# Gate weights by column halves, one visit for denominators and memory sums, and a new order of all work, in a mixed attention and feed-forward kernel

## The chip, the cores and the metric

The kernel runs on one core of one Trainium2 chip. TensorE (PE) multiplies, ScalarE (ACT) and VectorE (DVE) compute, GpSimd (POOL) and SyncE (SP) help, and DMA queues are fed by SP and ACT. The metric is the device time of one execution in microseconds, as the median of several runs. The inputs are bfloat16: a sequence of 2048 tokens with 512 features, four 512 by 512 attention weights, and the feed-forward weights of 512 by 1792, 512 by 1792 and 1792 by 512.

## The reference, cut to what matters

```python
q, k, v = ...                      # x @ wq, x @ wk, x @ wv, 32 heads of 16, 4 segments of 512 tokens
for s in range(4):
    p = softmax(q[s] @ k[s].T * 0.25 + causal_mask)
    a_dot = p @ v[s]
    pq = phi(q[s])                 # t + 1 where t > 0, else exp(t)
    a_mem = (pq @ M) / (pq @ z + 1e-6)
    o[s] = sigmoid(beta) * a_mem + (1 - sigmoid(beta)) * a_dot
    M = M + phi(k[s]).T @ v[s]
    z = z + phi(k[s]).sum(tokens)
a = o @ wo
b = (gelu(x @ w_gate) * (x @ w_up)) @ w_down
g = sigmoid((x * gate_w).sum(-1))
out = g * a + (1 - g) * b
```

In each segment of 512 tokens a causal softmax attention is mixed with a read of the memory M and its denominators z, which sum over earlier segments. A gated feed-forward runs on the same x, and a gate per token mixes the two results.

## The kernel before, in words

The work is cut into 1162 small tasks. Each names its engine, its instructions, and what it reads and writes. The string ORDER, written out at the end of the file, lists all tasks in one sequence. Every engine executes its own tasks in that sequence, and the emitter places a semaphore wait wherever a task reads what another engine wrote, or overwrites what another engine still reads. A digit behind a name says which of the four PSUM banks (or which turning buffer) the task takes, and `:a` or `:d` whether ACT or DVE copies a finished bank out. So the order decides where an engine has to wait.

For each segment s (0 to 3) these tasks matter here:

- `K`, `Q`, `V`, `G`, `U` with a segment and a tile number: dense products of x with the key, query, value, gate and up weights (line 483). A task is a pair of 512-column matmuls, `a` the first two input blocks and `b` the last two. Each product fills a bank that is then copied out by `Kev`, `Qev`, `Vev`, `Gev` (lines 475 and 476), by `gd` with the gelu in it (line 804), or multiplied on DVE by `h` (line 813). `gelu` (line 801) is the gelu of the first seven gate tiles in one instruction of 3584 columns.
- `st` with a segment, a quarter and a letter: a fill of the one score tile psX, which takes four of the eight banks, by four or eight small-tile matmuls side by side (line 634). `exp` (line 650, ACT) turns it into probabilities, `msk` (line 656, POOL) applies the causal triangle. The next fill may only start when that exponential has read psX.
- `pv` (line 687): 128 small-tile matmuls of probabilities and values into two banks, turned by DVE (`tp`, line 553), normalised (`pvp`), joined with the memory part and turned again (`ot`).
- `phq` and `phk`, each in three steps a, b, c (lines 493, 495, 496): the feature map phi of queries and keys on DVE, ACT and DVE. `ktr` (line 595) are four transposing DMAs, issued by SP, that bring the key features into token order.
- `mz` (line 602): 64 small-tile matmuls that form this segment's sums for M and z. `mzacc` (lines 608 and 609) adds them on DVE and scales M for the next read, `zq` (line 616) spreads z on POOL. `gate` (line 452) are 32 small matmuls for the token gates of two segments, in the same bank.
- `nz` (line 568): four small-tile matmuls for the denominators, in segments 1 to 3, turned by `tp_z` and inverted by `nzp`. `nd` (line 578) reads M into psX; four turns `tp_m` and four products `ndp` empty it, after which the next fill may start.
- `out`, `wev`, `wo`, `oev`, `dma` (lines 826 to 852): the down product, its scaling, the attention's output product, the sum, and the store. `chk` tests the softmax rows on DVE; `oksum` and `flag` join the tests, and every engine loads the flag at the end and branches on it.

The two kinds of visit of PE are of importance: dense products use the full array, while `st`, `pv`, `mz`, `nz`, `nd` and `gate` use tiles of 32 or 64 rows or columns.

Weights are loaded by SP in halves; each load names others that must have landed before it is issued. The gate weights `wg` come as `wg0` and `wg1`, each two of the four blocks of 128 input features with all 1792 columns, so a row of 3584 bytes each. The first two matmuls of a gate product read `wg0`, the last two `wg1`:

```python
ld_w("wg0", SP, wg[:, halves[0], :], wgr[:, halves[0], :], [("wg", 0)], 0.9, ["wq0"])
...
lambda i: [*x_of(s % R_XT, i), ("wg", i // 2)], 4)
```

At the start, PE runs `wake0` (five 512-column matmuls and three of 128 columns on constants) while the input lands, then turns x of the first segment (`xtr0_0` to `xtr0_3`, line 898), with one more filler, `wake1`, behind the second of these. `xev` copies the turned blocks out.

Of the kernel before, what the change touches and what calls it, by code (L numbers as in the profile page):

```python
# [12 lines left out]
ALU = mybir.AluOpType  # L13
# [239 lines left out]
def _build(es, nc, A_x, A_wq, A_wk, A_wv, A_wo, A_beta, B_w_gate, B_w_up, B_w_down, gate_w, out):  # L253
# [64 lines left out]
    def program(exact):  # L318
# [11 lines left out]
        def bk(s):  # L330
            return ("bank", s)
# [20 lines left out]
        def ld_w(name, eng, dst, src, writes, size, wait=()):  # L352
            load(name, eng, lambda e: e.dma_start(dst, src), writes, size=size, wait=[("ld", w) for w in wait])
# [20 lines left out]
        ld_w("wg0", SP, wg[:, halves[0], :], wgr[:, halves[0], :], [("wg", 0)], 0.9, ["wq0"])  # L374
        ld_w("wg1", SP, wg[:, halves[1], :], wgr[:, halves[1], :], [("wg", 1)], 0.9, ["wv"])
# [181 lines left out]
        def t_rows(ts, r):  # L557
            return tT[ts.i][:, :].rearrange("p (c r) -> p c r", r=32)[:, :, 0:r]
# [4 lines left out]
        def memory_read(s):  # L563
            b = s % 2
            for t0 in (0, 2):
                phi(s, "phq", qT[b], phq, t0, "qT")
            sl = Slot()
            one(f"nz{s}", PE, 0.24, [I(lambda e, c=c, sl=sl: e.matmul(  # L568
                BK[sl.i][32 * c:32 * c + 8, :], zq[:, c, :], phq[:, c, :], start=True, stop=True,
                tile_position=(0, 32 * c)), [("phq", c), ("zq",)], [bk(sl)]) for c in range(4)])  # L570
            ts = turn(f"{s}_z", lambda sl=sl: BK[sl.i][:, :], bk(sl))
            rv = rcm[:, :].rearrange("p (c r) -> p c r", r=8)
            one(f"nzp{s}", DVE, 1.15, [
                I(lambda e, rv=rv, ts=ts: e.tensor_scalar(rv, t_rows(ts, 8), EPS, None, ALU.add), [("tT", ts)], [("rcm",)]),
                I(lambda e: e.reciprocal(rcm[:, :], rcm[:, :]), [("rcm",)], [("rcm",)])])

            xs = Slot("X")
            one(f"nd{s}", PE, T_FILL, [I(lambda e, t=t, g=g, c=slot_of(t, g): e.matmul(  # L578
                XALL[quad(c), 512 * t:512 * t + 512], mzq[quad(g), c, :], phq[quad(g), c, :], start=True, stop=True,
                tile_position=(32 * g, 32 * c)), [("phq", slot_of(t, g)), ("mzq",)], [("X", xs)])  # L580
                for t in range(4) for g in range(4)], lat=0.27)
            for t in range(4):
                ts = turn(f"{s}_m{t}", lambda t=t: XALL[:, 512 * t:512 * t + 512], ("X", xs))
                f4 = lambda a: a.rearrange("p (c j e) -> p c j e", j=2, e=16)
                den = bass.AP(rcm, 2 * t, [[128, P], [8, 16], [1, 2], [0, 16]])
                one(f"ndp{s}_{t}", DVE, 0.61, [
                    I(lambda e, ts=ts, t=t, den=den: e.tensor_tensor(f4(omem[:, t, :]), f4(tT[ts.i][:, :]), den, ALU.mult),
                      [("tT", ts), ("rcm",)], [("omem", t)])])

        def memory_write(s):  # L590
            b = s % 2
            for t0 in (0, 2):
                phi(s, "phk", kT, phk, t0, "kT")
            for t in range(4):
                one(f"ktr{s}_{t}", SP, 1.3, [I(lambda e, t=t: e.dma_start_transpose(
                    phkt[:, :, t * 128:(t + 1) * 128], phk[:, t, :]), [("phk", t)], [("phkt", t)],
                    dma_sem=sem(f"s_k{s}_{t}"))]).size = 0.28

            sl = Slot()
            if s < 2:  # L600
                gate_products(s, sl)
            one(f"mz{s}", PE, 0.45, [I(lambda e, c=c, kt=kt, g=g, sl=sl: e.matmul(  # L602
                BK[sl.i][quad(g), 34 * c:34 * c + 34], phkt[:, kt, 128 * c + 32 * g:128 * c + 32 * g + 32],
                vnat[b][:, kt, :, 4 * c + g, :], start=(kt == 0), stop=(kt == 3), tile_position=(0, 32 * g)),
                [("phkt", c), ("vnat", b, kt)], [bk(sl)]) for c in range(4) for kt in range(4) for g in range(4)])
            acc = mzacc[:, :, :].rearrange("p c n -> p (c n)")
            one(f"mzacc{s}", DVE, 0.75, [
                I(lambda e, sl=sl: e.tensor_tensor(acc, BK[sl.i][:, 0:136], acc, ALU.add), [bk(sl), ("mzacc",)], [("mzacc",)]),
                I(lambda e: e.tensor_tensor(
                    mzq[:, :, :].rearrange("p c (j n) -> p (c j) n", j=2),  # L610
                    acc.rearrange("p (h n) -> p h n", n=17)[:, :, 0:16],
                    gphm[:, :, :].rearrange("p c (j o) -> p (c j) o", o=1).to_broadcast([P, 8, 16]), ALU.mult),
                    [("mzacc",), ("gphm",)], [("mzq",)])])
            if s < 2:
                gates(s, sl)
            one(f"zq{s}", POOL, 0.25, [I(lambda e: e.tensor_tensor(
                zq[:, :, :], mzacc[:, :, 16:17].to_broadcast([P, 4, 8]), zmask[:, :, :], ALU.mult),
                [("mzacc",), ("zmask",)], [("zq",)])])
# [170 lines left out]
        def glu_gate(s):  # L789
# [3 lines left out]
            for ft in range(NFT):  # L793
# [3 lines left out]
                           lambda i: [*x_of(s % R_XT, i), ("wg", i // 2)], 4)  # L797
# [112 lines left out]
        for s in range(NSEG):  # L910
            if s == 1:
                ld_xt(3)
            project(s)
            if s > 0:
                memory_read(s)
            if s < NSEG - 1:
                memory_write(s)
# [24 lines left out]
    def run(e, eng):  # L942
# [3 lines left out]
        em.emit(eng, slice(p.start + HINT[eng], p.stop - 1))  # L946
# [3 lines left out]
        em.emit(eng, slice(p.stop - 1, p.stop))  # L950
# [56 lines left out]
ident ld_x0_0 wake0:0 ld_x0_1 xtr0_0:3 xtr0_1 wake1 ld_wk0 ld_x0_2 xev0_1:d ld_wk1 xtr0_2 ld_wq0 xev0_0:a xev0_2:a  # L1007
xtr0_3 ld_wq1 K0_k0:2031 xev0_3:d ld_wv K0_k1 ld_beta K0_k2 ld_wg0 K0_k3 ld_wg1 K0_2b K0_3b ld_x1_2 Kev0_3:a Kev0_2:d
masks ld_x1_1 kpada0_2 consts K0_1b K0_0b Kev0_0:a causal0 Kev0_1:d Q0_3a:1 Q0_3b phka0_2 kpada0_3 Q0_2a:3 Q0_0a:0
kpadb0_1 kpadb0_3 kpada0_0 Qev0_3:a kpada0_1 phka0_0 Q0_0b Qev0_0:d phkb0_2 Q0_2b causal1 phkb0_0 ld_x1_0 Q0_1a:2  # L1010
Q0_1b Qev0_2:d Qev0_1:a kpadb0_0 kpadb0_2 V0_1a:0 V0_3a:3 st0_0A:0 V0_1b V0_2a:1 exp0_0A V0_0a:2 causal V0_2b vones0
V0_0b Vev0_2:d Vev0_1:d st0_0B:0 Vev0_0:a ld_x1_3 V0_3b G0_0a:1 G0_1a:2 G0_1b vsh0_00 Vev0_3:d G0_0b exp0_0B st0_0C:0
G0_2a:0 vsh0_21 G0_3a:3 Gev0_1:a G0_3b phkc0_0 Gev0_0:d vsh0_01 exp0_0C G0_2b ld_gw Gev0_3:a G1_6a:2 st0_0D:0 msk0_0B
Gev0_2:d vsh0_20 exp0_0D Q1_3a:1 G0_6a:0 ld_wu1 G1_6b Q1_3b ld_wo00 msk0_0C G0_6b Gev1_6:d msk0_0A st0_0E:0 Gev0_6:d
Qev1_3:a V1_0a:2 msk0_0D ld_wo10 betab Q1_2a:3 exp0_0E V1_3a:1 Q1_2b Qev1_2:d msk0_0E V1_3b st0_1A:0 Vev1_3:d V1_0b
exp0_1A K1_1a:3 K1_1b pv0_0:01 st0_1B:0 phqa1_2 Vev1_0:d Kev1_1:d K1_0a:2 tp0_d00:2 G0_5a:3 G0_5b G0_4a:0 ld_wo30
Gev0_5:d tp0_d01:0 phqb1_2 exp0_1B ld_x2_1 ktr0_1 G0_4b Gev0_4:d st0_1C:0 ld_wo11 msk0_1B K1_0b G1_1a:1 Kev1_0:d
exp0_1C G1_1b phkc0_2 ktr0_2 Q1_1a:3 V1_1a:0 Gev1_1:a st0_1D:0 exp0_1D K1_3a:2 K1_3b G0_8a:1 Kev1_3:d msk0_1D Q1_1b
V1_1b st0_2A:0 ktr0_3 ld_x2_2 Qev1_1:a msk0_1C G0_8b K1_2a:3 K1_2b Vev1_1:d bexp G0_10a:0 G1_7a:2 ld_wo01 G0_10b
exp0_2A Kev1_2:d G1_13a:3 msk0_2A gq G1_7b G1_13b gd0_8 msk0_1A gd0_10 gd1_13 G0_13a:1 pvp0_00 G0_13b ld_wu0 G0_9a:0  # L1020
gd1_7 G0_9b pv0_1:23 gd0_13 st0_2B:0 gd0_9 G0_7a:1 G0_7b tp0_d11:1 tp0_d10:2 G0_11a:0 pvp0_11 G1_9a:3 G0_11b kpadb1_2
ktr0_0 G1_8a:2 G1_9b G1_8b gelu0 gd0_11 kpadb1_3 kpadb1_1 gd0_7 G0_12a:0 gd1_8 gd1_9 G0_12b gph U0_8a:1 U0_8b U0_9a:2
gd0_12 h0_8 U0_11a:3 Q1_0a:0 U0_9b exp0_2B pvp0_01 phka1_2 phka1_0 kpada1_1 msk0_2B U0_3a:1 ld_wd0 phkb1_2 U0_3b h0_9
U0_11b h0_3 Q1_0b st0_2C:0 Qev1_0:d G1_5a:1 exp0_2C h0_11 G1_5b gate0:2 pvp0_10 mz0 Gev1_5:a st0_2D:0 kpada1_2 U0_1a:0
V1_2a:3 ld_wo21 mzacc0 U0_4a:1 V1_2b ld_x2_0 phqa1_0 kpada1_0 gz0 Vev1_2:d U0_4b ld_x2_3 h0_4 exp0_2D kpadb1_0
st0_2E:0 exp0_2E U0_5a:2 U0_1b U0_5b U0_7a:3 h0_5 U0_7b msk0_2C st0_3A:0 h0_1 exp0_3A U0_6a:1 h0_7 U0_6b msk0_2D
# [88 lines left out]
```

## Time and profile before

| what | value |
|---|---|
| median of 3 runs | 265.61 us (265.2 to 265.67) |
| the profiled execution: its time | 265.43 us |
| the profiled execution: its span, first to last instruction | 263.7 us |
| PE busy | 254.1 us (96%) |
| ACT busy | 208.7 us (79%) |
| DVE busy | 206.7 us (78%) |
| POOL busy | 96.7 us (37%) |
| share of PE in the chain that ended last | 94% |
| data read, written | 8.14 MB, 2.10 MB |

The span is the part that the profile sees; 1.73 us of the execution lie outside it. Busy times are unions of instructions, so instructions that overlap on an engine count once. The chain is followed back from the last instruction: at each step to what released it.

### The profile page before, as it was taken

What the parts mean: (1) busy time and instruction counts of PE and PEld (TensorE: products, weight loads), DVE (VectorE), ACT (ScalarE), POOL (GpSimd) and SP (SyncE); (2) the same over time, 40 slices, a digit from 0 to 9 for tenths busy, and PEclk for the clock granted to TensorE, in tenths of its full rate; (3) what the DMA queues carried; (4) which work ended last, traced back from release to release, by engine and by line L of the source; (5) the groups of instructions that cost most, each with busy time, mean ns of one, the idle gap of its engine ahead of it and who ended that gap; (6) DMA issues with size and microseconds to landing.
All of it is one profiled execution on the core that took longest, in us unless ns stands there. A gap on an engine that the chain in (4) does not pass through costs nothing.

```text
span 263.7 us, 6612 instructions
## 1 busy us (share of the span) xinstructions
PE 254.1 (96%) x2792; PEld 113.2 (43%) x2830; DVE 206.7 (78%) x392; ACT 208.7 (79%) x169; POOL 96.7 (37%) x159
## 2 busy tenths in 40 slices
PE   7999999999999999999999999999999999999996
PEld 4634444444343443544434344444344443444443
DVE  1764853799969658989998899796989697968965
ACT  3589799988888989999778798668889967476512
POOL 6015342053532633142263545523543035163500
PEclk9999999999999999999999999999999999999999
DMA  6995169910026110000002200010002000010002
GB/s 225 255 216 166 42 94 201 253 62 4 0 63 96 42 42 20 2 4 20 2 0 57 67 2 2 20 43 10 4 2 74 2 2 0 2 60 2 20 2 86
DMA packets 24159, 14.96 MB, mean 57 GB/s; under 512 B 14526, under 2 KB 23102, under 8 KB 24126
## 3 DMA queue, kind: packets, MB, share of 16 engines
q1 hardware_dynamic: 23566, 14.04, 23.3%
q8 instruction: 23, 0.38, 0.6%
q10 hardware_dynamic: 560, 0.46, 0.5%
q14 instruction: 10, 0.08, 0.1%
HBM read 8.14 MB, written 2.10 MB: 39 GB/s over the span
## 4 chain that ended last, share of the span: by engine, by line
PE 94%; issue 2%; DMA 2%; DVE 0%; ACT 0%; SPq 0%
PE psD L483 52%; PE psD L826 19%; PE psX L634 9%; PE psD L687 6%; PE psD L843 5%; DMA pt<-in_A_x_dram 2%; PE psD L602 1%; PE psD L511 1%; PE psD L505 1%; PE psD L452 0%; PE psX L578 0%; PE psD L568 0%; DVE ost L847 0%; PE psX L898 0%; ACT vnat L475 0%
## 5 line engine op out<-in xcount | busy, mean ns | idle before, releaser
L650 ACT ACTIVATE pt<-psX 128x2048 bf16<-128x2048 f32 x72 | 135.1, 1876 | 32.7 <-PE psX L634 31.0
L656 POOL TENSOR_TENSOR pt<-pt,ctri 128x256 bf16<-128x256 bf16 x128 | 91.4, 719 | 152.0 <-ACT pt L650 147.4
L483 PE MATMUL psD<-xT,wu 128*128 128x512 bf16 x215 | 54.2, 380 | 1.4 <-issue 0.9
L483 PE MATMUL psD<-xT,wg 128*128 128x512 bf16 x211 | 52.7, 379 | 1.6 <-issue 1.4
L826 PE MATMUL psD<-wd,gb 128*128 128x512 bf16 x219 | 53.4, 380 | 0.6 <-issue 0.3
L813 DVE TENSOR_TENSOR gb<-psD,gb 128x512 bf16<-128x512 f32 x56 | 37.3, 683 | 11.8 <-PE psD L483 11.3
L826 PEld LDWEIGHTS psD<-wd,gb 128*128 128x128 bf16 x224 | 20.7, 98 | 26.0 <-issue 2.8
L483 PEld LDWEIGHTS psD<-xT,wg 128*128 128x128 bf16 x224 | 20.5, 98 | 26.1 <-issue 2.4
L553 DVE STREAM_TRANSPOSE tT<-psD 128x512 f32<-128x512 f32 x35 | 23.6, 697 | 10.1 <-PE psD L687 9.5
L483 PEld LDWEIGHTS psD<-xT,wu 128*128 128x128 bf16 x224 | 20.3, 98 | 26.0 <-issue 3.4
L634 PE MATMUL psX<-qT,kD 32*128 32x192 bf16 (+7 forms) x512 | 28.5, 287 | 0.0
L699 DVE SCALAR_TENSOR_TENSOR ob<-tT,gq,rcall 128x256 bf16<-128x256 f32 x32 | 17.9, 559 | 1.1
L687 PE MATMUL psD<-pt,vnat 64*17 64x128 bf16 (+7 forms) x512 | 18.8, 283 | 0.0
L634 PEld LDWEIGHTS psX<-qT,kD 32*128 32x128 bf16 x512 | 8.2, 92 | 24.4 <-ACT pt L650 19.8
L687 PE MATMUL psD<-pt,vsh 64*17 64x128 bf16 (+7 forms) x512 | 18.2, 283 | 0.0
L483 PE MATMUL psD<-wv,xT 128*128 128x512 bf16 x62 | 17.4, 380 | 0.2 <-issue 0.2
L483 PE MATMUL psD<-xT,wq 128*128 128x512 bf16 x62 | 17.0, 379 | 0.2 <-issue 0.2
L476 DVE CAST gb<-psD 128x512 bf16<-128x512 f32 x18 | 12.1, 681 | 6.4 <-PE psD L483 6.3
L847 DVE SCALAR_TENSOR_TENSOR ost<-psD,gtok,wds 128x512 bf16<-128x512 f32 (+1 forms) x18 | 12.2, 686 | 6.0 <-PE psD L843 5.8
L843 PE MATMUL psD<-wo,oT 128*128 128x512 bf16 (+1 forms) x68 | 15.3, 354 | 0.6 <-issue 0.6
L804 ACT ACTIVATE gb<-psD 128x512 bf16<-128x512 f32 x28 | 15.0, 603 | 0.7 <-PE psD L483 0.6
L687 PEld LDWEIGHTS psD<-pt,vnat 64*17 64x17 bf16 x512 | 11.6, 86 | 8.9 <-issue 4.1
(102 smaller groups left out, 256.9 us busy)
## 6 DMA issues: line engine op xcount, KB each, us to landing
out_dram<-ost SPq DMA_DIRECT2D x15, 128.0 KB, 1.7
wg<-in_B_w_gate_dram SPq DMA_DIRECT2D x2, 896.0 KB, 6.9
wu<-in_B_w_up_dram SPq DMA_DIRECT2D x2, 896.0 KB, 5.5
wd<-in_B_w_down_dram SPq DMA_DIRECT2D x2, 896.0 KB, 8.1
vsh<-vnat SPq DMA_DIRECT2D x16, 68.0 KB, 2.3
wq<-in_A_wq_dram SPq DMA_DIRECT2D x2, 256.0 KB, 5.1
wv<-in_A_wv_dram SPq DMA_DIRECT2D x1, 512.0 KB, 4.5
wk<-in_A_wk_dram ACTq DMA_DIRECT2D x1, 256.0 KB, 4.4
```

The lines of the kernel that those rows point to most:

```text
L483: one(f"{name}{'abcd'[h // 2]}", PE, 2 * T_MM, [I(lambda e, i=i: e.matmul(BK[sl.i][:, :], lhs(i), rhs(i), start=(i == 0), stop=(i == n - 1 ...
L553: one(f"tp{name}", DVE, 0.605, [I(lambda e, ts=ts, bank=bank: e.transpose(tT[ts.i][:, :], bank()), [key], [("tT", ts)])])
L634: ins.append(I(lambda e, c=c, kb=kb, ncol=ncol, c0=c0, g=g: e.matmul(XALL[:, g * 512 + c0:g * 512 + c0 + ncol], kD[b][quad(g), c, kb, :], ...
L650: one(f"exp{s}_{name}", ACT, 2048 * 0.000833 + 0.05, [I(lambda e: e.activation(pt[slot][:, :, :], xin, ACTF.Exp, scale=ATT_SCALE), [("X", ...
L656: ins.append(I(lambda e, mv=mv: e.tensor_tensor(mv, mv, cm, ALU.mult), [("pt", slot), ("causal",)], [("pt", slot)]))
L687: ins.append(I(lambda e, kb=kb, slot=slot, c0=c0, n=n, g=g, c=c, r0=r0, sl=banks[j], va=va: e.matmul(BK[sl.i][32 * c:32 * c + 17, 64 * kb: ...
L699: I(lambda e, ts=ts, t=t, j=j, dst=dst, r=r: e.scalar_tensor_tensor(out=dst, in0=t_rows(ts, 16), scalar=gq[:, 2 * t + j:2 * t + j + 1], in ...
L804: one(f"gd{s}_{ft}", ACT, 0.485, [I(lambda e, gi=gi, f=f, sl=sl: e.activation(gb[gi][:, f, :], BK[sl.i][:, :], ACTF.Gelu_apprx_tanh), [bk( ...
L813: one(f"h{s}_{ft}", DVE, 0.605, [I(lambda e, sl=sl, gi=gi, f=f: e.tensor_tensor(gb[gi][:, f, :], BK[sl.i][:, :], gb[gi][:, f, :], ALU.mult ...
L826: mm.append(I(lambda e, fb=fb, gi=gi, f=f, q=q, sl=sl: e.matmul(BK[sl.i][:, :], gb[gi][:, f, q], wd[:, fb, :], start=(fb == 0), stop=(fb = ...
L843: one(f"wo{s}_{qt}_{ci}", PE, 4 * T_MM / len(parts), [I(lambda e, kb=kb, q=q, so=so, c=c: e.matmul(BK[so.i][:, c], oT[:, kb, q], wo[:, kb, ...
L847: lambda e, so=so, gt=gt, wi=wi, oi=oi, c=c: e.scalar_tensor_tensor(out=ost[oi][:, c], in0=BK[so.i][:, c], scalar=gtok[:, gt:gt + 1], in1= ...
```

## The change

The diff has four parts.

First, the two loads of the gate weights are cut by columns: `wg0` holds columns 0 to 895 of all four blocks, `wg1` the rest, in rows of 1792 bytes. A gate tile of the first seven now reads `wg0` alone, one of the last seven `wg1` alone.

Second, `memory_read` and `memory_write` become one function `memory`. In segments 1 and 2 the four denominator matmuls (formerly task `nz`) stand right behind the 64 matmuls of the sums, in one PE task `mz`; in segment 3, which has no sums, `mz3` is the denominators alone. The gate products of segments 2 and 3 are formed in the visit of segment 2 instead of segment 1. The two DVE instructions of `mzacc` become two tasks, `mzacc` and `mzm`, so that M can be scaled for the next read after the current read is done.

Third, at the end of the program every engine's last task, the load of the flag, comes ahead of SP's wait for the first fourteen stores instead of behind it.

Fourth, ORDER is new from the first task to the last, engines and banks included: 42 instead of 38 copies out of PSUM fall to ACT and 54 instead of 58 to DVE. Some stretches that differ are shown, each cut from the two lists.

```diff
-        ld_w("wg0", SP, wg[:, halves[0], :], wgr[:, halves[0], :], [("wg", 0)], 0.9, ["wq0"])
-        ld_w("wg1", SP, wg[:, halves[1], :], wgr[:, halves[1], :], [("wg", 1)], 0.9, ["wv"])
+        ld_w("wg0", SP, wg[:, :, 0:DF // 2], wgr[:, :, 0:DF // 2], [("wg", 0)], 0.9, ["wq0"])
+        ld_w("wg1", SP, wg[:, :, DF // 2:DF], wgr[:, :, DF // 2:DF], [("wg", 1)], 0.9, ["wv"])
...
-                           lambda i: [*x_of(s % R_XT, i), ("wg", i // 2)], 4)
+                           lambda i, h=ft // HFT: [*x_of(s % R_XT, i), ("wg", h)], 4)
...
-            one(f"nz{s}", PE, 0.24, [I(lambda e, c=c, sl=sl: e.matmul(
...
+        def memory(s):
             b = s % 2
+            read, write = s > 0, s < NSEG - 1
+            visit = []
...
+            if write:
...
+                if s % 2 == 0:
+                    gate_products(s // 2, sw)
+                visit += [I(lambda e, c=c, kt=kt, g=g: e.matmul(
+                    BK[sw.i][quad(g), 34 * c:34 * c + 34], phkt[:, kt, 128 * c + 32 * g:128 * c + 32 * g + 32],
+                    vnat[b][:, kt, :, 4 * c + g, :], start=(kt == 0), stop=(kt == 3), tile_position=(0, 32 * g)),
+                    [("phkt", c), ("vnat", b, kt)], [bk(sw)]) for c in range(4) for kt in range(4) for g in range(4)]
+            if read:
+                sr = Slot()
+                visit += [I(lambda e, c=c: e.matmul(
+                    BK[sr.i][32 * c:32 * c + 8, :], zq[:, c, :], phq[:, c, :], start=True, stop=True,
+                    tile_position=(0, 32 * c)), [("phq", c), ("zq",)], [bk(sr)]) for c in range(4)]
+            one(f"mz{s}", PE, 0.24 * read + 0.45 * write, visit)
...
-        em.emit(eng, slice(p.start + HINT[eng], p.stop - 1))
+        em.emit(eng, slice(p.start + HINT[eng], p.stop))
...
-        em.emit(eng, slice(p.stop - 1, p.stop))
...
-ident ld_x0_0 wake0:0 ld_x0_1 xtr0_0:3 xtr0_1 wake1 ld_wk0 ld_x0_2 xev0_1:d ld_wk1 xtr0_2 ld_wq0 xev0_0:a xev0_2:a
+wake0:0 ld_x0_0 ld_x0_1 ld_wk0 ld_x0_2 wake1 ident xtr0_1 xtr0_0:3 xev0_1:a xtr0_2 xev0_0:d xtr0_3 ld_wk1 xev0_2:d
...
+st0_0D:0 Gev0_2:a exp0_0D Gev0_3:d G0_6b msk0_0B G1_6a:3 V1_3a:1 msk0_0A ld_wo00 Gev0_6:d G1_6b st0_0E:0 ld_wo10
...
+G1_11a:2 phqc1_2 kpada2_0 phka2_0 wev0_0:d msk1_0C msk1_0D gelu1 wo0_1_0:3 G1_11b wev0_1:d vsh1_21 out0_3_4 oev0_1_0
+msk1_0E gd1_11 K2_2a:0 wev0_3:d K2_2b st1_1A:0 vsh1_20 pv1_0:12 Kev2_2:d mz1:30 exp1_1A tp1_d00:2 mzacc1 st1_1B:0
...
```

More of the change, by code (lines that the diff above doesn't have):

```diff
@@ L590, in memory_write @@
[L590 to L618, printed above, removed]
@@ new lines, in memory @@
+            if read:
+                sr = Slot()
[3 more added lines that the diff above has]
+            one(f"mz{s}", PE, 0.24 * read + 0.45 * write, visit)
+            if read:
+                ts = turn(f"{s}_z", lambda: BK[sr.i][:, :], bk(sr))
+                rv = rcm[:, :].rearrange("p (c r) -> p c r", r=8)
+                one(f"nzp{s}", DVE, 1.15, [
+                    I(lambda e, rv=rv, ts=ts: e.tensor_scalar(rv, t_rows(ts, 8), EPS, None, ALU.add), [("tT", ts)], [("rcm",)]),
+                    I(lambda e: e.reciprocal(rcm[:, :], rcm[:, :]), [("rcm",)], [("rcm",)])])
+                xs = Slot("X")
+                one(f"nd{s}", PE, T_FILL, [I(lambda e, t=t, g=g, c=slot_of(t, g): e.matmul(
+                    XALL[quad(c), 512 * t:512 * t + 512], mzq[quad(g), c, :], phq[quad(g), c, :], start=True, stop=True,
+                    tile_position=(32 * g, 32 * c)), [("phq", slot_of(t, g)), ("mzq",)], [("X", xs)])
+                    for t in range(4) for g in range(4)], lat=0.27)
+                for t in range(4):
+                    ts = turn(f"{s}_m{t}", lambda t=t: XALL[:, 512 * t:512 * t + 512], ("X", xs))
+                    f4 = lambda a: a.rearrange("p (c j e) -> p c j e", j=2, e=16)
+                    den = bass.AP(rcm, 2 * t, [[128, P], [8, 16], [1, 2], [0, 16]])
+                    one(f"ndp{s}_{t}", DVE, 0.61, [
+                        I(lambda e, ts=ts, t=t, den=den: e.tensor_tensor(f4(omem[:, t, :]), f4(tT[ts.i][:, :]), den, ALU.mult),
+                          [("tT", ts), ("rcm",)], [("omem", t)])])
@@ new lines, in memory @@
+            if write:
+                acc = mzacc[:, :, :].rearrange("p c n -> p (c n)")
+                one(f"mzacc{s}", DVE, 0.75, [
+                    I(lambda e: e.tensor_tensor(acc, BK[sw.i][:, 0:136], acc, ALU.add), [bk(sw), ("mzacc",)], [("mzacc",)])])
+                one(f"mzm{s}", DVE, 0.3, [
+                    I(lambda e: e.tensor_tensor(
+                        mzq[:, :, :].rearrange("p c (j n) -> p (c j) n", j=2),
+                        acc.rearrange("p (h n) -> p h n", n=17)[:, :, 0:16],
+                        gphm[:, :, :].rearrange("p c (j o) -> p (c j) o", o=1).to_broadcast([P, 8, 16]), ALU.mult),
+                        [("mzacc",), ("gphm",)], [("mzq",)])])
+                if s % 2 == 0:
+                    gates(s // 2, sw)
+                one(f"zq{s}", POOL, 0.25, [I(lambda e: e.tensor_tensor(
+                    zq[:, :, :], mzacc[:, :, 16:17].to_broadcast([P, 4, 8]), zmask[:, :, :], ALU.mult),
+                    [("mzacc",), ("zmask",)], [("zq",)])])
@@ L913, in program @@
             project(s)
[L914 to L917, printed above, removed]
+            memory(s)
             if exact:
@@ L1032 @@
-out0_1_1 exp1_0D out0_1_2 vsh1_00 Vev2_3:d st1_0E:0 zq0 gr0 pvp0_20 exp1_0E out0_1_3 Q2_3a:1 pvp0_31 out0_1_4 go0
-wev0_1:a Q2_3b st1_0C:0 exp1_0C ot0_2 K2_3a:2 vsh1_01 Qev2_3:d K2_3b pvp0_30 out0_3_0:1 gd1_11 msk1_0B ktr1_1 ktr1_0
-ot0_3 out0_3_1 st1_1A:0 phka2_0 out0_3_2 ktr1_2 out0_3_3 gelu1 msk1_0C ld_wo20 msk1_0D out0_3_4 exp1_1A out0_0_0:3
-out0_0_1 msk1_0E msk1_0A vsh1_21 wo0_1_0:0 out0_0_2 chk0 vsh1_20 Kev2_3:d ktr1_3 out0_0_3 oev0_1_0 wev0_3:d out0_0_4
-wev0_0:d K2_2a:0 K2_2b Kev2_2:a pv1_0:12 st1_1B:0 tp1_d00:2 nz1:3 wo0_0_0:0 tp1_d01:1 tp1_z:0 exp1_1B Q2_1a:1 G2_4a:2
@@ new lines @@
+pvp1_11 G2_9a:3 G2_1b G2_0a:1 G2_0b exp1_2C dma0_0 ktr2_0 kpada2_2 Gev2_0:d st1_2D:0 G2_12a:0 Gev2_1:a ndp1_2
+wo0_2_0:2 kpadb2_0 G2_13a:1 msk1_2C oev0_2_0 exp1_2D pvp1_10 msk1_2A G2_12b phqa2_2 G2_13b gd2_13 mzm1 st1_2E:0 G2_9b
+G2_8a:2 gd2_12 G2_8b wo0_3_0:1 kpadb2_2 chk0 oev0_3_0 ot1_1 gd2_9 V2_0a:3 U1_8a:0 U1_8b gd2_8 V2_0b U1_1a:1 h1_8
+U2_5a:2 U2_5b msk1_2D Q2_0a:0 Vev2_0:d gelu2 exp1_2E Q2_0b ktr2_1 U1_1b U1_3a:3 U1_3b h2_5 Qev2_0:d U1_7a:2 h1_1 U1_7b
+msk1_2E U1_5a:1 st1_3A:0 U1_0a:0 h1_3 U1_5b h1_7 ot1_0 U1_0b h1_5 exp1_3A pv1_2:23 st1_3B:0 phkb2_2 h1_0 tp1_d21:1
```

176 lines of the change are left out of this document (80 added, 96 removed).

## The prediction

> **What bounds the kernel now.** The first page first: its row of busy times and, among the forty slices, the row of PE.
>
> ```profile
> PE 254.1 (96%) x2792; PEld 113.2 (43%) x2830; DVE 206.7 (78%) x392; ACT 208.7 (79%) x169; POOL 96.7 (37%) x159
> ...
> PE   7999999999999999999999999999999999999996
> ```
>
> Only the first and the last slice are not full. Busy shares can hide pauses, so the list of waits comes next, for what PE itself waited:
>
> ```profile
> PE psD L483 <- issue: 3.2, 20, 0.2
> ...
> PE psX L392 <- PEq L1100: 0.8, 1, 0.8
> ...
> PE psX L898 <- DMA pt<-in_A_x_dram: 0.5, 1, 0.5
> ```
>
> The first row is twenty pauses of 0.16 us, each the way back from small tiles to the full array; the other two lie before 5.5 us. There is no row in which PE waited for a gate weight. To be sure, I add up PE's work by the spacing of starts in the timeline. A 512-column matmul takes 0.2158 us; the kernel has 928 of them (halves counted as halves): 200.3. A score fill is priced here, with the timeline of PE and ACT:
>
> ```profile
> 21.55 0.40 PE L634 MATMUL psX<-qT,kD 32*128 32x320 bf16 x8
> ...
> 22.00 1.88 ACT L650 ACTIVATE pt<-psX 128x2048 bf16<-128x2048 f32 x1 [0.23 <-PE psX L634]
> ...
> 24.14 0.40 PE L634 MATMUL psX<-qT,kD 32*128 32x256 bf16 x8
> ```
>
> From fill to fill 2.59 us with ten matmuls between, so a fill costs 2.595 - 2.158 = 0.437: 72 of them are 31.5. A value visit beside a fill adds 1.10 (26.73 to 29.56 with six matmuls), fifteen of them 16.5, the lonely last one 1.44. Memory sums 0.65, denominators 0.32, reads 0.50 (three of each), gate products 0.51 (two), eight transposes 0.45: 5.9. Sum 255.6. The chain of waits runs on PE from 5.41 to 260.65, which is 255.2. So this stretch holds no stall that an order could remove, within a few tenths. Ahead of it lie 5.4 us in which the input lands, behind it 3.0 us of last evictions and stores, and 265.43 - 263.7 = 1.73 us outside the span. The profiled execution's 265.43 is the base of my sum; the median of the runs is 265.61, 0.18 higher.
>
> The same timeline gives the one limit that paces PE. The exponential starts 0.45 after its fill, runs 1.88, and the next fill starts 0.06 later at the earliest (197.61 to 197.66). So fills cannot follow one another in under 2.39 us. Nine matmuls give 0.437 + 1.942 = 2.38, just enough, and the old order holds such a place:
>
> ```profile
> 230.77 0.40 PE L634 MATMUL psX<-qT,kD 32*128 32x384 bf16 x8
> ...
> 233.15 0.40 PE L634 MATMUL psX<-qT,kD 32*128 32x320 bf16 x8
> ```
>
> Eight give 2.16, and PE would wait 0.23.
>
> **The change, part by part.** *Gate weights.* The view of tile wg:
>
> ```profile
> L483 PE MATMUL psD<-xT,wg x5: 379/379/379, 17.1 to 18.0; 128*128 128x512 bf16 x5
> L353 SPq DMA_DIRECT2D wg<-in_B_w_gate_dram x2: 368/368/368, 7.3 to 9.9; - x2
> ...
> DMA to landing us min/median/max: 6.7/6.9/7.1
> ```
>
> The halves land at 7.32 + 7.1 = 14.4 and 9.93 + 6.7 = 16.6; the first gate matmul is at 17.1, the first that reads the second half is the fifth, at 18.0. After the change the first seven feature tiles need only the first half, and the second is read 76 matmuls and nine fills later. The margin grows from 1.4 us to over 15, but PE waited for neither: 0. Bytes are the same; rows of 1792 instead of 3584 bytes lie between the 3584-byte packets (183 ns each in the trace) and the 1024-byte ones (52 ns), both some 19.7 bytes per ns, so the landing moves by little against 2.7 us of cover. If that half came 3 us late, PE would lose 0.3. SP's issue may rise from 0.37 to the 0.58 of the seven-block loads; what is behind it, the transposing loads of x, is read over 2 us after landing (the first such product moves behind the fill of 21.55). Value taken: 0.
>
> *Merged visits.* No matmul is removed. Counting PE's tasks in the two lists, alternations between dense and small-tile work fall from 76 to 75, since the old denominators already stood beside a fill. The one that goes is at st1_1A, pv1_0, mz1, st1_1B, now one block. The four matmuls of a fill run side by side in the time of one, 0.22 of its 0.437, and the lonely value visit is 0.34 dearer than one beside a fill, so the gain is 0.21 to 0.34; I take 0.25. The new wait is that denominators follow the 64 sums, which wait for four transposed feature tiles. In the old run the last of these for segment 1 is issued at 83.4 and lands near 87, and the new visit comes near 92; SP's queue ahead of it holds the same loads. In segment 2 the visit moves from 195.6 to about 160 and needs its second feature pass on DVE by then; the DVE tasks listed between pv2_0 and it end about 2 us earlier. Behind a late visit all of PE would queue; cover 2 to 5 us, so 0. The gate products of segments 2 and 3 move with it, read first near 220: 0. The split of the sum's update leaves the same two DVE instructions: 0.
>
> *The order.* I counted matmuls between fills in the new list. Most gaps have ten or more, four of the closing ones nine (0.01 each), values with four matmuls 0.437 + 1.10 + 0.86 = 2.40, enough. One is short: st0_0D to st0_0E has eight: **+0.23**. A second: from st1_0C to st1_1A stand 37 matmuls, then the merged block. ACT must there end one exponential (2.33 after the fill), load a table (1.28), run the wide gelu (3.19), then gd1_11, whose matmuls end 30 matmuls in, at 7.1; then 0.6, a table (1.28), 1.88 and 0.06: 10.9. PE is there after 0.437 + 7.98 + 2.27 = 10.7: **+0.23**, which eats the visit saved. A third: two evictions ahead of exp1_2C put it 0.1 to 0.15 behind: **+0.13**. The other three gelu blocks hold as many matmuls as before (66 and 58) or two fewer (52 for 54, where ACT's chain, 12.1, just equals PE's).
>
> *Front and tail.* The chain ahead of 5.41 is the landing of the third input block, whose place in SP's queue is unchanged; transposing the second block first costs 0.17 and is done at 4.9, still hidden. In the tail 36 matmuls instead of 33 follow the last value visit, DVE's test of rows moves ahead of two evictions, and both last stores stay behind the same evictions. SP's flag read no longer waits for the fourteenth store, but the last store landed at 263.2, later than both: 0.
>
> **Sum:** 265.43 - 0.25 + 0.23 + 0.23 + 0.13 = 265.77, so **265.8**.
>
> **The rivals.** *A, slower: DVE falls behind around the second memory read.* From pvp1_00 to ot1_1 the new list gives DVE 28 tasks (six turns, four memory products, four kD halves and others) that make 16.6 us by the spacing of their starts and 19.7 by their mean durations, beside 14.9 us of PE. The old list's worst such stretch has 15.75 beside 15.8. The first fill after the read waits for the four turns (0.4 to spare), and Q2_0a waits for a bank that h1_8 frees just behind ot1_1 (0.45 to spare by the short spacings). It decides once DVE is over 0.45 late there: with spacings halfway to the means the stretch is 18.1, 1.5 longer, so 1.0 is lost: 266.8, and from 266.3 to 267.2 by the share. For it: the old run has DVE busy for 3.96 of the 4.0 us ahead of its own read (100 to 104), and its row test took 1.8 us at 85.4 for 1.08 by the mean. Against it: walking down the list by the short spacings, I find DVE pausing 0.75 there for G2_0b, which takes up part of a delay.
>
> *B, slower: the filler matmul moves.* It stood at 4.64 between transposes and now follows the other fillers. Spacing of 128-column matmuls is 107 ns up to 4.44 and 56 from 5.41. If the rate doubles later, the sixteen key matmuls from 6.03 (1.75 us) take 1.9 times as long: +1.6, 267.4. The profile's granted clock reads 1.00 from 0 to 8 us and so shows nothing of this. The Trainium skill (TensorE: Matmul & The Clock Gate, Part 1) says that the clock doubles after a window of about 3.4 us of activity that runs free of the program; the spacings agree with the doubling, no row shows the window. One filler of 0.1 us is little activity, hence a small chance.
>
> *C, faster: landings were late after all.* If executions differ by late landings (265.2 to 265.67), an order with more margin would take the lowest, and with the visit saved and none of the stalls above it gives 265.2 - 0.25 = 264.95. Against it: PE's waits list no landing after 5.5 us.
>
> *That the change does not do what it says* is part of the forecast: the merging saves one alternation, not three.
>
> **How the numbers follow.** Forecast 0.50, A 0.36, B 0.03, C 0.11. A measurement of this kernel can tell about 0.2% from no change, 0.53 us. The forecast is within it (265.8 against 265.6), A and B above, C below. The range reaches from C to the upper end of A and leaves out B and the far ends: 264.9 to 267.2. The forecast's own range is 265.4 to 266.1.
>
> **What would show it.** st0_0E should start 0.06 behind the exponential before it, and likewise st1_1B; the chain of waits should stay on PE from 5.41 to about 261. Rival A shows as PE waiting for DVE between 110 and 125 us, B as 107 ns spacing past 5.41, C as a span below 263.3. I am wrong if PE waits over 0.3 us at any one place that I did not name.

## The result, and the profile after

The changed kernel takes 267.17 us (median of 9 executions, 266.33 to 268.72) where the kernel before, run beside it, takes 265.61. The ratio is 1.0058, with a 95% interval of 1.0034 to 1.0083: so the changed kernel is slower by 0.3 to 0.8%. The time lies inside the range on record, near its upper end, but the likeliest case there was 265.8, "no change", and the rival that would have given 267 (DVE falling behind) did not happen.

The profiled execution of the changed kernel takes 266.56 us, its span is 264.8; that of the kernel before takes 265.43 and 263.7. First the first page, as before: busy time and the row of PE in the forty slices.

```profile
PE 259.7 (98%) x2830; PEld 113.3 (43%) x2830; DVE 202.1 (76%) x388; ACT 210.2 (79%) x173; POOL 97.1 (37%) x159
...
PE   8999999999999999999999999999999999999994
```

PE is as full as it was, and the list of what PE waited for is shorter. These are all its rows:

```profile
PE psX L392 <- PEq L1102: 0.8, 1, 0.8
PE psX L903 <- DMA pt<-in_A_x_dram: 0.4, 2, 0.2
```

Both lie before 6 us. That points away from the body of the kernel. To find the loss I cut both traces at the same instructions: the start of the first score fill (st0_0A), the start of the last output product on PE (the last matmul of `wo`), and the end of the span. PE's very last matmul would not do, since in the kernel before it is the one of the flag's test, and in the changed kernel that one comes earlier.

| stretch | before | changed | difference |
|---|---|---|---|
| start to first score fill | 13.77 | 13.84 | +0.07 |
| first score fill to last output product | 247.01 | 247.06 | +0.05 |
| last output product to end of span | 2.91 | 3.93 | **+1.02** |
| outside the span | 1.74 | 1.74 | 0 |

The whole new order, 247 us of it, costs 0.05 us. Nearly all of the loss lies behind the last output product, where ACT and DVE do the same work at nearly the same moments, the flag apart: DVE's last sum ends at 261.57 before and at 261.69 now. What differs is the landing of the last stores. The issues of the DMA view from 260 to 266 us, with KB each and the median time from issue to landing, kernel before:

```profile
out_dram<-ost SPq DMA_DIRECT2D x1, 64.0 KB, 1.6
out_dram<-ost ACTq DMA_DIRECT2D x1, 64.0 KB, 1.6
```

Changed kernel, same view:

```profile
out_dram<-ost SPq DMA_DIRECT2D x1, 64.0 KB, 2.8
out_dram<-ost ACTq DMA_DIRECT2D x1, 64.0 KB, 2.6
```

SP waits for these two, and for the store ahead of them, at the very end. Its row in the list of waits (us in total, times, longest) reads, before and then changed:

```profile
SPq L983 <- DMA out_dram<-ost: 0.5, 1, 0.5
```

```profile
SPq L984 <- DMA out_dram<-ost: 1.3, 1, 1.3
```

In the trace every store counts sixteen landings, one for each DMA engine. Before, the sixteen parts of the last store land from 263.01 to 263.19. In the changed kernel fifteen land from 263.17 to 263.34 and the sixteenth at 264.32; of the store before it, fifteen by 263.13 and one at 264.12. One DMA engine was busy with something else. The DMA view of the changed kernel from 262.05 to 262.35 us names it (queue, kind, packets, MB):

```profile
q1 hardware_dynamic: 29, 0.02, 19.3%
q8 instruction: 1, 0.02, 18.3%
```

The second row is one packet of 16384 bytes of program code. It starts at 262.06 and takes 0.88 us on one engine, and the data packets queued behind it there start when it ends. In the kernel before the same window holds data alone:

```profile
q1 hardware_dynamic: 141, 0.06, 73.8%
```

There that packet starts at 263.42, behind the last landing. It follows PE: in both traces it starts 0.7 us after the end of PE's branch at the end of the program (261.37 in the changed kernel, 262.73 before). And PE branches early now because the flag on which every engine branches is known early. DVE's copy of it, in the timeline of the kernel before and of the changed one:

```profile
261.49 0.13 DVE L727 COPY flag<-psD 1x1 f32<-1x1 f32 x1
```

```profile
259.46 0.14 DVE L732 COPY flag<-psD 1x1 f32<-1x1 f32 x1 [1.58 <-PE psD L730]
```

Theory F is, then: the order puts the test of rows and the flag 2 us earlier; PE, no longer held by them, leaves the program right behind its last matmul; its code fetch comes ahead of the last two stores on one DMA engine and holds one sixteenth of them back by 1 us.

### The profile page after: what moved, and what is told of

Its sections match the earlier page's. It is cut to its first block, busy times and chain, and to the rows that moved or that the text cites. A ratio compares the mean times of both kernels' runs of the same rounds, so it can differ in the third digit from the quotient of the medians.

```text
span 264.8 us, 6664 instructions
## 1 busy us (share of the span) xinstructions
PE 259.7 (98%) x2830; PEld 113.3 (43%) x2830; DVE 202.1 (76%) x388; ACT 210.2 (79%) x173; POOL 97.1 (37%) x159
## 4 chain that ended last, share of the span: by engine, by line
PE 96%; DMA 1%; ACT 1%; DVE 0%; SPq 0%; issue 0%
PE psD L483 52%; PE psD L831 19%; PE psX L639 9%; PE psD L692 7%; PE psD L848 5%; DMA pt<-in_A_x_dram 1%; ACT pt L655 1%; PE psD L580 1%; PE psD L505 1%; PE psD L511 1%; PE psD L452 0%; PE psX L598 0%; PE psX L903 0%; DVE ost L852 0%; PE psD L586 0%; SPq L353 0%
## 5 line engine op out<-in xcount | busy, mean ns | idle before, releaser
L483 PE MATMUL psD<-xT,wu 128*128 128x512 bf16 x224 | 56.0, 380 | 0.0
L483 PE MATMUL psD<-xT,wg 128*128 128x512 bf16 x224 | 54.9, 380 | 0.0
L831 PE MATMUL psD<-wd,gb 128*128 128x512 bf16 x224 | 54.4, 380 | 0.0
L836 ACT ACTIVATE wds<-psD,omgt 128x512 f32<-128x512 f32 x10 | 6.9, 686 | 13.2 <-PE psD L831 12.1
L848 PE MATMUL psD<-wo,oT 128*128 128x512 bf16 (+1 forms) x72 | 16.2, 356 | 0.0
```

The costliest lines, as they stand in the source:

```text
L483: one(f"{name}{'abcd'[h // 2]}", PE, 2 * T_MM, [I(lambda e, i=i: e.matmul(BK[sl.i][:, :], lhs(i), rhs(i), start=(i == 0), stop=(i == n - 1 ...
L831: mm.append(I(lambda e, fb=fb, gi=gi, f=f, q=q, sl=sl: e.matmul(BK[sl.i][:, :], gb[gi][:, f, q], wd[:, fb, :], start=(fb == 0), stop=(fb = ...
L848: one(f"wo{s}_{qt}_{ci}", PE, 4 * T_MM / len(parts), [I(lambda e, kb=kb, q=q, so=so, c=c: e.matmul(BK[so.i][:, c], oT[:, kb, q], wo[:, kb, ...
```

## The experiments

Eleven runs were made in three groups, each beside the kernel before on its chip (medians of the latter: 265.53, 265.66 and 265.20). Traces of single executions are cut as above; the cuts of all of them are in a table at the end.

**1. The flag put back to the end of the changed order.**

```diff
-wo3_1_0:3 out3_2_4 out3_3_2 out3_3_3 oev3_0_0 out3_3_4 oev3_1_0 wev3_2:a oksum:2 wo3_2_0:3 dma12_0 flag wo3_2_1:0
-oev3_2_0 oev3_2_1 wev3_3:a wo3_3_0:2 wo3_3_1:3 dma13_0 oev3_3_0 oev3_3_1 dma15_1 dma14_1 dma15_0 reg_pe reg_act
+wo3_1_0:3 out3_2_4 out3_3_2 out3_3_3 oev3_0_0 out3_3_4 oev3_1_0 wev3_2:a wo3_2_0:3 dma12_0 wo3_2_1:0
+oev3_2_0 oev3_2_1 wev3_3:a wo3_3_0:2 wo3_3_1:3 dma13_0 oev3_3_0 oev3_3_1 dma15_1 dma14_1 oksum:1 flag dma15_0 reg_pe reg_act
```

> The changed kernel with the flag's matmul and copy (oksum, flag) put back to the end of the order, behind the last output products and sums; nothing else differs. Theory F (the program's code is fetched over the DMA engines the last stores use: the flag, known 2 us earlier, lets PE and the others reach their branch early, and PE's fetch of 16384 bytes, 0.88 us on one DMA engine, comes ahead of the last two stores): the fetch starts behind the last landing again, the last two stores land in 1.6 to 1.7 us instead of 2.6 to 2.8, the span is 263.6 to 263.9, the time 265.3 to 265.7, about 1.1 us (0.4%) below the changed kernel's profiled execution. Rival R (the changed kernel's longer tail is chance, or the loss lies elsewhere, in the front or in the order): time and span as of the changed kernel, 266.4 to 267.2.

Measured: 265.70, ratio 1.0001 (0.9983 to 1.0019). The loss is gone. The execution that was profiled is by chance the longest of the thirteen (267.57), yet its tail is short: 3.02 us, with the fetch at 265.36 behind the last landing at 265.15.

```profile
out_dram<-ost SPq DMA_DIRECT2D x1, 64.0 KB, 1.6
out_dram<-ost ACTq DMA_DIRECT2D x1, 64.0 KB, 1.6
```

Its 2 us stand at the start instead: the first score fill is at 15.73 (more on that below).

**2. The flag put early in the kernel before.** The old order otherwise, old loads, old visits.

```diff
-wev3_1:a tp3_d30:2 tp3_d31:1 out3_2_4 pvp3_30 pvp3_31 out3_3_0:1 out3_3_1 ot3_3 wo3_0_0:0 oev3_0_0 wo3_1_0:3 oev3_1_0
-out3_3_2 dma12_0 out3_3_3 chk3 wev3_2:a out3_3_4 okrow wo3_2_0:0 oev3_2_0 wo3_2_1:3 oev3_2_1 wo3_3_0:2 dma13_0
-wev3_3:a wo3_3_1:0 oev3_3_0 oev3_3_1 dma14_1 dma15_1 oksum:3 flag dma15_0 reg_pe reg_act reg_dve reg_pool reg_sp
+wev3_1:a tp3_d30:2 tp3_d31:1 out3_2_4 pvp3_30 pvp3_31 out3_3_0:1 out3_3_1 ot3_3 chk3 okrow wo3_0_0:0 oev3_0_0 wo3_1_0:3 oev3_1_0
+out3_3_2 dma12_0 out3_3_3 wev3_2:a out3_3_4 oksum:2 wo3_2_0:0 flag oev3_2_0 wo3_2_1:3 oev3_2_1 wo3_3_0:2 dma13_0
+wev3_3:a wo3_3_1:0 oev3_3_0 oev3_3_1 dma14_1 dma15_1 dma15_0 reg_pe reg_act reg_dve reg_pool reg_sp
```

> The kernel before with the test of rows and the flag put early, as the changed kernel has them (chk and okrow ahead of the first output product of the last segment, oksum behind the third); nothing else differs. Theory F: PE's fetch of 16384 bytes starts near 262.1, before the last stores have landed, one of the sixteen parts of each of the last two stores lands 0.9 to 1.1 us behind the others, the span is 264.6 to 265.0 and the time 266.3 to 267.0. Rival R: 265.4 to 265.8, as before.

Measured: 266.73, ratio 1.0057 (1.0036 to 1.0079), the whole loss of the change in a kernel that has nothing else of it. The fetch starts at 261.41, and the last two stores land in 2.8 and 2.6 us, in the trace as in the changed kernel. The rival, that the longer tail was chance or the loss lay elsewhere, falls with these two runs.

**3. Flag last, and two pairs of matmuls moved** to fill the stall that I had counted at st0_0E.

```diff
-st0_0D:0 Gev0_2:a exp0_0D Gev0_3:d G0_6b msk0_0B G1_6a:3 V1_3a:1 msk0_0A ld_wo00 Gev0_6:d G1_6b st0_0E:0 ld_wo10
-K1_1a:2 V1_3b V1_0a:0 Gev1_6:d V1_0b exp0_0E msk0_0C K1_1b ld_wo30 bexp ld_x2_1 st0_1A:0 Q1_3a:3 msk0_0D Q1_3b
+st0_0D:0 Gev0_2:a exp0_0D Gev0_3:d G0_6b msk0_0B G1_6a:3 V1_3a:1 msk0_0A ld_wo00 Gev0_6:d G1_6b K1_1a:2 st0_0E:0 ld_wo10
+V1_3b V1_0a:0 Gev1_6:d V1_0b exp0_0E msk0_0C K1_1b ld_wo30 bexp ld_x2_1 Q1_3a:3 st0_1A:0 msk0_0D Q1_3b
```

> As the first, and one pair of matmuls moved ahead of st0_0E (K1_1a) and one ahead of st0_1A (Q1_3a), so that ten matmuls stand between st0_0D and st0_0E instead of eight. By my count of matmuls the stall of 0.22 us at st0_0E goes and four matmuls beside the value visit behind st0_1A are enough: 0.2 us below the first, 265.1 to 265.5. If PE's stalls are only taken back at the next limit (the value visit waits for probabilities, or the wide gelu later), it is equal to the first.

Measured: 265.52, ratio 1.0003 (0.9991 to 1.0016). In the trace the stall of 0.22 us is gone and half of it is back three fills later, where the fill at 32.21 starts 0.10 late; the middle stretch is 246.91 against 247.02 in the first run. That is too little for a measured time to show.

**4. The gate weights alone**, in the old order.

```diff
-        ld_w("wg0", SP, wg[:, halves[0], :], wgr[:, halves[0], :], [("wg", 0)], 0.9, ["wq0"])
+        ld_w("wg0", SP, wg[:, :, 0:DF // 2], wgr[:, :, 0:DF // 2], [("wg", 0)], 0.9, ["wq0"])
...
-                           lambda i: [*x_of(s % R_XT, i), ("wg", i // 2)], 4)
+                           lambda i, h=ft // HFT: [*x_of(s % R_XT, i), ("wg", h)], 4)
```

> The kernel before with the gate weights loaded and read by column halves, in the old order. As predicted: 0, 265.4 to 265.8, with the landings of the two halves within 1 us of the old ones and no wait of PE for them. If rows of 1792 bytes landed much later than rows of 3584, PE would wait for the first gate product or for other loads behind them: 266 or more.

Measured: 265.77, ratio 1.0012 (0.9987 to 1.0037): nothing that can be told. The halves land 6.7 and 6.9 us after issue, 6.7 and 7.1 before.

**5. The filler matmul back in its old place**, the rest as changed.

```diff
-wake0:0 ld_x0_0 ld_x0_1 ld_wk0 ld_x0_2 wake1 ident xtr0_1 xtr0_0:3 xev0_1:a xtr0_2 xev0_0:d xtr0_3 ld_wk1 xev0_2:d
+wake0:0 ld_x0_0 ld_x0_1 ld_wk0 ld_x0_2 ident xtr0_1 xtr0_0:3 wake1 xev0_1:a xtr0_2 xev0_0:d xtr0_3 ld_wk1 xev0_2:d
```

> The changed kernel with the filler matmul wake1 put back between the second and the third transposed block, where it stood before; flag early, as changed. Theory F (the fetch ahead of the last stores is the whole loss): as the changed kernel, 266.6 to 267.2. Rival B of the prediction (without that filler the rate of PE doubles later): 56 ns spacing of 128-column matmuls from 5.2 to 5.5 us instead of past 5.85, and 0.2 to 0.5 us less than the changed kernel run beside it, with fewer executions far above the median.

Measured: 266.94, ratio 1.0043 (1.002 to 1.0067). The loss stays, and so does the late part: of the store before the last fifteen parts have landed by 263.21 and one at 264.46. The short spacing does not come at 5.2 to 5.5 but only at 6.5, so the filler alone does not set it.

**6. The changed kernel once more.**

> The changed kernel itself once more, as a measure for its neighbours and for a second profile. 266.9 to 267.3; PE's fetch ahead of the last landings again, and one of sixteen parts of the last two stores behind the rest by about 1 us. If theory F is chance of one execution, this profile shows the last two stores landing in 1.7 us.

Measured: 266.32, ratio 1.0036 (1.0011 to 1.0062). The median is lower than expected, but the second profile shows the same tail: fetch at 261.70, fifteen parts of the last store by 262.93, the sixteenth at 264.11.

**7. SP's waits for fourteen stores back ahead of its flag load** (the third part of the change undone).

```diff
-        em.emit(eng, slice(p.start + HINT[eng], p.stop))
+        em.emit(eng, slice(p.start + HINT[eng], p.stop - 1))
         if eng == SP:
             for name in outs[:-3]:
                 e.wait_ge(sem(name), 16)
+        em.emit(eng, slice(p.stop - 1, p.stop))
```

> The changed kernel with the third part of the change undone: SP waits for the first fourteen stores ahead of its load of the flag, as before. SP is not the engine whose fetch blocks the stores, so both theories say no change against the changed kernel: 266.8 to 267.3. If SP's own early branch and fetch made the loss, 265.5 to 266.

Measured: 267.07, ratio 1.0063 (1.0037 to 1.0089). As both theories said: SP's own place is not the cause.

**8. Run 3 with the filler back and four times as long.**

```diff
-        for i, cols in enumerate(([512] * 5 + [128] * 3, [128] * 1)):
+        for i, cols in enumerate(([512] * 5 + [128] * 3, [128] * 4)):
```

> The kernel with the flag last and the two pairs moved, with wake1 back between the second and third transposed block and made of four 128-column matmuls instead of one. If the gap ahead of the third block's landing is what lets PE's rate double late, the doubling comes by 5.2 us in every execution: 265.0 to 265.4 and no execution above 266. If landings alone set the front: 265.5, as without fillers.

Measured: 265.59, ratio 1.0003 (0.998 to 1.0027), with one execution at 267.86. No gain: in its trace 128-column matmuls still start 107 ns apart up to 5.70. My expectation missed: the fillers do not fix the moment of the doubling.

**9 and 10. Who must be held?** In both the flag is as early as in the changed kernel, and some engines load it only when the last sum is written. For that the loads are made into a function that is called behind the outputs; run 9 holds PE alone, run 10 the counterpart, ACT, DVE and POOL.

```diff
+                late = [("ost", 1, 1)] if eng == PE else []
+                one(f"reg_{eng}", eng, 0.1, [I(lambda e, eng=eng: fetch(e, eng), [("flag",), *late])])
-                one(f"reg_{eng}", eng, 0.1, [I(lambda e, eng=eng: fetch(e, eng), [("flag",)])])
```

```diff
+                late = [("ost", 1, 1)] if eng in (ACT, DVE, POOL) else []
```

> The changed kernel, flag early as changed, with one wait added: PE loads the flag only when the last sum (oev3_3_1) is written, near 261.7; the other engines load it as early as the change lets them. Theory F with PE's fetch of 16384 bytes as the cause: PE branches near 262.7 and fetches near 263.4, behind the last landing; the last two stores land in 1.6 to 1.8 us, time 265.4 to 265.9, about 1 us below the changed kernel. If the other engines' fetches of 8192 bytes each (POOL's near 261.3) make the loss: as the changed kernel, 266.3 to 267.2. If the loss were the mere order of the flag on DVE or PE: unchanged as well.

> The counterpart: ACT, DVE and POOL load the flag only when the last sum is written, PE and SP as the change has them. Theory F with PE's fetch as the cause: the fetch of 16384 bytes still starts near 262.1 or earlier, one of sixteen parts of the last two stores lands 1 us late, 266.3 to 267.2. If the other engines' fetches make the loss: 265.4 to 265.9.

Measured, PE held: 265.59, ratio 1.0023 (1.0001 to 1.0046). Others held: 267.01, ratio 1.009 (1.0057 to 1.0123). The DMA view from 260 to 266 us, PE held:

```profile
out_dram<-ost SPq DMA_DIRECT2D x1, 64.0 KB, 1.9
out_dram<-ost ACTq DMA_DIRECT2D x1, 64.0 KB, 1.7
```

Others held:

```profile
out_dram<-ost SPq DMA_DIRECT2D x1, 64.0 KB, 2.8
out_dram<-ost ACTq DMA_DIRECT2D x1, 64.0 KB, 2.6
```

One added wait on PE alone takes most of the loss away; holding the three others, whose fetches are packets of 8192 bytes, leaves all of it. The packet of 16384 bytes goes along: with PE held it starts at 262.95, as the last part lands, with the others held at 261.71. So it is PE's code, and it is the cause.

Run 9's interval still lies just above 1, and its tail is 0.25 us longer than that of the kernel before (3.16 and 2.91). Of this 0.17 stands behind the last landing, and goes with the third part of the change. SP's waits for fourteen stores now come behind its load of the flag, so its branch comes later: it ends at 262.67, and SP's wait for the last three stores starts 0.47 later, at 263.14, while the last part has landed at 262.95. In the kernel before, SP stands at that wait when the part lands (263.19). Runs 1, 3, 8 and 11 show the same: in each SP's last wait starts 0.47 behind its branch and 0.13 to 0.17 behind the landing. Run 7 undoes the third part but cannot show this, since its landing is late; no run has the flag last and the waits back. The other 0.08 of run 9 stands ahead of the landing. POOL's packet at 260.85 to 261.39 lies beside the third-last store (1.9 us to landing for 1.7); that is a reading, not a test.

**11. Run 9 with the two pairs of run 3**, all that the runs point to.

> The ninth run's kernel with the two pairs moved as in the third (K1_1a ahead of st0_0E, Q1_3a ahead of st0_1A): the version with all that the runs point to. 265.3 to 265.7, equal to the kernel before within what can be told, since PE's stream is then only 0.1 us shorter than before. If an early release of the other engines shortens the end, up to 0.3 below the kernel before.

Measured: 265.72, ratio 1.0011 (0.9992 to 1.0029), 0.02 above the range expected. The middle stretch is 246.94, 0.07 below the kernel before, and 246.91 in the two other runs with the pairs (3 and 8); that is below what a time can show. No version here is measurably faster than the kernel before.

The cuts of all profiled executions, in us: from the start to the first score fill, from there to the last output product, and from there to the end (the tail). "PE's fetch" is the start of the last packet of 16384 bytes, "landing" the last part of the last store.

| run | first fill | to last output product | tail | PE's fetch | landing |
|---|---|---|---|---|---|
| before | 13.77 | 247.01 | 2.91 | 263.42 | 263.19 |
| changed | 13.84 | 247.06 | 3.93 | 262.06 | 264.32 |
| 1 flag last | 15.73 | 247.02 | 3.02 | 265.36 | 265.15 |
| 2 before, flag early | 13.22 | 247.03 | 3.93 | 261.41 | 263.69 |
| 3 flag last, pairs | 14.15 | 246.91 | 3.02 | 263.68 | 263.46 |
| 4 gate columns | 14.14 | 247.01 | 2.90 | 263.80 | 263.55 |
| 5 filler back | 13.97 | 247.05 | 4.15 | 262.19 | 264.67 |
| 6 changed again | 13.47 | 247.05 | 4.09 | 261.70 | 264.11 |
| 7 end waits back | 15.56 | 247.06 | 4.09 | 263.80 | 266.21 |
| 8 flag last, fillers | 13.90 | 246.91 | 3.02 | 263.43 | 263.22 |
| 9 PE held | 13.40 | 247.07 | 3.16 | 262.95 | 262.95 |
| 10 others held | 13.47 | 247.06 | 3.93 | 261.71 | 263.97 |
| 11 PE held, pairs | 14.18 | 246.94 | 3.07 | 263.90 | 263.53 |

The tail column falls into two groups with nothing between 3.16 and 3.93: the fetch stands ahead of the landing in each of the upper group and in none of the lower. The first column scatters by 2.5 us, in one and the same kernel too (13.84 and 13.47 for the changed one). The medians show the tail only roughly: those of the upper group lie 0.7 to 1.8 us above the kernel before, their tails 1.0 to 1.2. What makes up the rest was not tested.

## Why the prediction was right and wrong, point by point

**What bounds the kernel: right.** PE's stream bounds it in every run: from the first fill to the last output product all thirteen profiles lie within 0.2 us. One reading was wrong without harm: the twenty "issue" pauses of 0.16 us were no way back from small tiles. The changed kernel's list has none of them in a stretch of the same length. The first page of before counts 2792 matmul records, that of changed 2830; run 1, with the changed kernel's matmuls, counts 2794 and has the pauses again. They are matmuls whose record is missing.

**Gate weights, 0: right**, by run 4 alone.

**Merged visits and order on PE, +0.34 in sum: too high by 0.29**, as the stretch became 0.05 longer. One stall was where and as large as I said. In the timeline of the changed kernel the exponential behind st0_0D and the fill st0_0E:

```profile
22.07 1.88 ACT L655 ACTIVATE pt<-psX 128x2048 bf16<-128x2048 f32 x1
...
24.00 0.40 PE L639 MATMUL psX<-qT,kD 32*128 32x256 bf16 x8
```

The fill starts 0.06 behind the end of the exponential (22.07 + 1.88 = 23.95, by the unrounded times 23.94), and 0.53 behind the last matmul where 0.31 is usual: 0.22, forecast 0.23. The other two were over-counted. At st1_1B PE stands 0.07 us instead of 0.23 (0.377 from denominators to fill, 0.311 where nothing waits), and at st1_2D it does not stand at all, though ACT is 0.17 late there: a slack of 0.27 behind ten matmuls took it up. The three stalls make 0.29 instead of 0.59. What is left, 0.05 - 0.29 = -0.24, is the saved visit (forecast -0.25) with all smaller shifts, among them the flag's matmul, which the new order puts into this stretch (0.03: with it put back in run 1 the stretch is 247.02). I did not measure the saved visit alone.

**Front, 0: right in size** in the profiled pair (+0.07), **but by luck**. Timeline of PE, before and then changed, at the transposes of the third input block:

```profile
5.41 0.62 PE L898 MATMUL psX<-ident,pt 128*128 128x128 bf16 x8 [0.55 <-DMA pt<-in_A_x_dram]
```

```profile
5.03 1.03 PE L903 MATMUL psX<-ident,pt 128*128 128x128 bf16 x8 [0.22 <-DMA pt<-in_A_x_dram]
```

The block came 0.38 sooner, and the eight transposes took about as much longer, because PE still ran at half rate (107 ns apart up to 5.85). That spacing past 5.41 is the sign that the prediction named for rival B.

**Tail, 0: wrong, and this is the step that failed.** The prediction says of the tail that "DVE's test of rows moves ahead of two evictions, and both last stores stay behind the same evictions", that the last store landed later than SP's flag read, and therefore 0. I asked whether any work in the tail would start later. None does. I did not ask what the earlier flag sets free: five engines' branches, and behind PE's a fetch of 16384 bytes on a DMA engine that the last stores still need. The term is +1.02 in the profiled pair. The sum by measured terms is 265.43 + 0.07 + 0.05 + 1.02 = 266.57, beside the profiled 266.56. The move of SP's waits, also put at 0, costs 0.1 to 0.2 us where the stores land in time, as in run 9. The profile of before had the hint: its DMA queues hold instruction packets, and the flag's copy is the last DVE instruction of the run, so the engines' way out was waiting for it.

**Rival A (DVE behind at the second read): did not happen.** Between 108 and 126 us PE's list of waits has no row, and that of its weight loads has none for DVE. The time in its range came from another place, so the range held by luck.

**Rival B (filler moved): wrong as a cause, though its sign and its price were seen.** In run 7 the sixteen key matmuls run at half rate, in run 6, the same front, at full rate. Timeline of PE, run 7 and then run 6:

```profile
5.94 3.62 PE L505 MATMUL psD<-xT,wk 128*128 128x256 bf16 x16
```

```profile
5.57 1.91 PE L505 MATMUL psD<-xT,wk 128*128 128x256 bf16 x16
```

That is 1.7 us, near the 1.6 that I had given, but it comes and goes between executions of one kernel, and with the filler back (run 5) or four of them (run 8) the short spacing came only at 6.5 and 5.8 us. A late doubling also stands in the two longest profiled executions (267.57 in run 1, 268.56 in run 7), and is the likely reason why single executions pass 267.3 with all of these kernels but that of run 3, the one before included. So only medians over many executions and tails cut out of the trace could be compared.

**Rival C (late landings cost): did not happen**; the run with the flag last has the new loads and equals the kernel before.

## What to carry to other kernels

When a change makes a signal earlier, ask what it releases, not only what it delays: here an early end of program brought a code fetch ahead of the last stores. At the end of a kernel let the engine whose code comes in the large packets, here PE, branch when the last stores are under way, by making it wait for the last piece of work, and look at whether all sixteen parts of a store land together. Cut two traces at the same instructions before explaining a difference: three cuts showed that 247 of 265 us had hardly changed.

## What the runs showed of the hardware

PE's code comes in packets of 16384 bytes; the one at the end of the program took 0.88 to 1.39 us on one DMA engine. Those of the other engines, by their places behind those engines' branches, are of 8192 bytes and took 0.3 to 0.8 us there. The delayed data packets begin when PE's code packet has ended: at 262.77 us in run 6, where it ran from 261.70 to 262.77; eight of one store follow, and then eight of the other. The Trainium skill (DMA: Bandwidth & Descriptors, Queues, rings and completion order) says that a DMA engine takes turns between its queues packet by packet and finishes a whole packet first; the trace agrees, and shows what that costs when the packet is a block of code. The Trainium skill (Runtime: NRT & Kernel Launch, Instruction fetch mechanics) says that code is refilled in blocks of 16 KiB, whose cost is mostly hidden. The size agrees for PE and not for the other engines' 8192 bytes, and the cost was not hidden here: it fell on the last stores, 1.0 us.

The rate of PE doubled between 4.0 us (run 9) and 9.4 us (run 7) after the start, and the first score fill lies between 13.22 and 15.73 us accordingly, together with the landings of the input. Twelve of the thirteen traces hold a record of the granted clock, and in each it begins within the step, or the pause of PE, in which the spacing of the matmuls halves: at 5.99 us in the changed kernel, at 3.97 in run 9, at 9.44 in run 7. The views read 1.00 ahead of it as well, because no record stands there. The record lasts 259.413 us in eleven traces and 256.000 in run 7, which is 76 and 75 times 3.4133 us; one of 0.5 follows it.

The Trainium skill (TensorE: Matmul & The Clock Gate, Part 1), which the prediction weighed, speaks of a window of some 3.4 us that runs free of the program. The lengths of these records agree with such a window. So the rate does not double after some amount of work, but where a window ends: in run 7 PE works without a gap from 5.12 to 9.36, 4.2 us, at half rate, and the window that ends at the doubling is the one from 6.03 to 9.44. By an estimate from the starts and the spacing of the matmuls, PE was busy for three quarters or more of the window that ends at the doubling in all twelve (0.75 to 1.0), and for less in every window ahead of it (at most 0.74). That would explain why fillers do not fix the moment: they do not move the windows. What share is needed was not tested.
